# Local attention and an exact-weight MLP on one Trainium2 core: dummy transposes in planned pauses, a second buffer for late probabilities, and early transposes in another PSUM pool

## The chip, the cores and the metric

The kernel runs on one core of one Trainium2 chip. A core has a matrix engine (TensorE; PE in the profile, with its weight loads as PEld), a vector engine (VectorE, DVE), a scalar engine (ScalarE, ACT) and GpSimd (POOL). SyncE (SP) issues the DMAs. SBUF is the working memory; PSUM is the small memory that TensorE writes its results to, and here it is divided into four pools (s, o, h, a) of two buffers each. The metric is device time in microseconds; lower is better.

## The reference: what is computed

Attention over 4 batches, 8 heads, 768 positions and head size 64. Each position sees the keys less than 16 positions away, and 24 summaries of the whole sequence (the maximum of each block of 32 keys, the mean of each block of 32 values). Then layer norm and an MLP with a hidden width of 2048 are applied to the 512 joined channels, with a residual:

```python
    k_sum = k.reshape(B, H, nb, block, D).max(axis=3)
    v_sum = v.reshape(B, H, nb, block, D).mean(axis=3)
    scores_l = scale * np.matmul(q, k.transpose(0, 1, 3, 2))
    mask_l = np.abs(pos[:, None] - pos[None, :]) < window
    scores_s = scale * np.einsum('bhsd,bhnd->bhsn', q, k_sum) + np.log(block)
    scores_all = np.concatenate([np.where(mask_l, scores_l, -1e9), scores_s], axis=-1)
    a = softmax(scores_all)
    x = np.matmul(a, np.concatenate([v, v_sum], axis=2))
...
    xn = (x - mu) / np.sqrt(var + 1e-06) * g_ln
    ch = np.maximum(xn @ w_ch1, 0.0) @ w_ch2
    return (x + ch).astype(np.float32)
```

(The softmax and the joining of the heads are shortened here.) The MLP weights reach the kernel as pairs of 32-bit words, from which it rebuilds float32 values.

## The kernel before

**Tiling.** The 4 x 768 rows make 24 tiles of 128 rows. Attention works on half tiles, t = 0 to 47: four heads of one row tile each. Two row tiles make a group (12 groups), and the MLP works on groups: `g1(s)` computes 256 hidden channels of a group (24 matmuls into a PSUM tile named h) and splits the result into two float16 parts, hh (ScalarE) and hl (VectorE). `g2(s)` multiplies both parts by the second weights into accumulators named a. A float32 product is formed from float16 parts: a high part and a low remainder on each side.

**Stages.** Half tiles 0 to 11 (batch 0, `NEARLY` = 12) take an early path in float32: scores (`early_qk`, PSUM tile s), softmax, transposes of the probabilities on TensorE (`early_transp`, PSUM tile pp, copied by ScalarE to pT), the product with the values (`early_pv`, tile o), then layer norm (`ln`) and its transposed copy (`lnT`, tile tx, then xs). Meanwhile the MLP weights are decoded by `dec_w` (tiles raw and wf), scaled by `scale_w` (tiles wps and wsc) and split into float16 parts by `conv_w` (wp), mostly on VectorE and ScalarE. Half tiles 12 to 47 take the late path: float16 parts of queries, keys and values, and probabilities that are split by ScalarE and GpSimd in `transp` (p16) and transposed by DMA.

**What sets the order.** All steps are recorded by a planner (`Plan`), which knows a cost for each operation and a waiting time between engines. Nothing is written down as an order by hand: `schedule` is a list scheduler over all five engines, `improve` runs it `ROUNDS` = 32 times, forward and backward in turn, and keeps the order with the earliest planned end. `issue` then emits every instruction in order of its planned start. On the chip each engine works through its own queue in that order and waits by semaphore. The planner has a model of TensorE's clock: in ticks of 10240/3 ns it counts columns, and where a tick held fewer than 3200, matmuls take twice as long in the next one. Any change of a dependency or a cost thus lets the planner order all engines anew.

**Buffers.** A PSUM pool's two buffers are handed round in the order in which the program allocates them, so a tile has to wait until the tile two before it in its pool has been read. Pool h holds the warm-up tile, pp of half tiles 0 to 3 (`EH` = 4, two pp per half tile), then wps and the h tiles. Pool s holds the scores, and pp from half tile 4 on, and tx from row tile 2 on. Pool a holds v0, the first two tx tiles, and the accumulators. In SBUF, a work tile with the name of an older one takes its place once that one has been read. Late keys (ksg) rotate over the three places `ksg=("qke", "k0_0", "k0_1")`. Early probabilities alternate between `prob[0]` and `prob[1]`; late ones all use `prob[0]`, by this line of `softmax`:

```python
            st[t, "p"] = prob[t < NEARLY and t % 2]
```

**Lines that the steps touch.** `warm` issues 36 transposes of an identity matrix ahead of everything else (`WARM`), `early_transp` picks the pool by `t < EH`, `go_late` clears the pads of the late buffers, `transp` is what reads the late probabilities (two casts on ScalarE, two subtractions on GpSimd). In the profile every instruction carries the line of the planner's emitting loop, L349, so the tile names tell the steps apart.

Of the kernel before, what the change touches and what calls it, by code (L numbers as in the profile page):

```python
# [23 lines left out]
P = 128  # L24
# [5 lines left out]
NC = 184  # L30
NE = 192
# [4 lines left out]
NEARLY = 2 * NT  # L36
# [1 line left out]
PET = 4  # L38
HB = 9
XSCALE, W1TOP, W2TOP, SQ = 4.0, 2.0**9, 2.0**15, 2.0**-24  # L40
EH = 4
BS = 3
ROUNDS = 32
WARMQ = 4
# [8 lines left out]
RAWS += [f"w{m}" for m in range(10, 16)] + ["ring0", "ring1"] + [f"w{m}" for m in range(12, 16)]  # L53
RAWS += [f"ring{m}" for m in range(4)]
AWAY = 24
LOADS = [("fetch_k0", 0), ("fetch_k0", 1), ("fetch_q", 0), ("gain",), ("fetch_blocks",), ("fetch_k0", 2), ("fetch_k0", 3)]
LOADS += [("fetch_v0", c) for c in range(7)] + [("fetch_tail", 0), ("fetch_q", 1), ("fetch_tail", 1), ("fetch_tail", 2)]
NV = 3
HOMES = dict(
    ksg=("qke", "k0_0", "k0_1"),  # L60
    kh=("kh0", "kh1", "kx0", "kx1"),
    qs=("qs", "qw0"),
    p16=("p2", "k0_2"),
# [32 lines left out]
class Plan:  # L96
# [10 lines left out]

    def __init__(self):
        self.ops, self.slots, self.prev, self.uses = [], {}, {}, {}
        self.joined = False  # L110
        self.names, self.stage = [("", ())], 0
        for e in self.ENGINES:
            setattr(self, e, Plan.Queue(self, e))
# [125 lines left out]
    def waits(self, x):  # L239
# [7 lines left out]
                wait.append((j, self.slack(x, y) + (self.LAND.get(n, 1000) if y.engine == "sync" else self.WAIT[y.engine])))  # L247
        return wait

    def slack(self, x, y):  # L250

        name, a = self.names[x.stage]
        if x.engine == "tensor":
            if name in ("g1", "g2"):
                return SLACK2 * (a[0] >= 24)
            return SLACK * (name in ("qk", "pv", "batch_s"))
        late = name in ("load_q", "load_k", "load_v", "softmax", "transp", "pv") and a[0] >= LATE
        late |= name[:5] == "batch" and a[0] >= 2
        late |= name in ("ln", "lnT") and a[0] >= LATE // 2
        late |= name in ("g1", "g2") and a[0] >= 24  # L260
        if not late:
            return 0.0
        return SLACKD if y.engine == "sync" else SLACKE

    def schedule(self, rank, after, back):

        count = len(self.ops)
        before = [[] for _ in range(count)]
        left = [len(x) for x in after]
        for i, x in enumerate(after):  # L270
            for j, wait in x:
                before[j].append((i, wait))
        ready, start, end = [0.0] * count, [0.0] * count, [0.0] * count
        free = dict.fromkeys(self.ENGINES, 0.0)
        coming, waiting = ({e: [] for e in self.ENGINES} for _ in range(2))
        ring, warm, columns, tick = 0.0 if back else self.FIRST, False, 0.0, 0.0
        port, half = 0.0, 0
        for i in range(count):
            if not left[i]:
                heapq.heappush(coming[self.ops[i].engine], (0.0 if back else 1000.0, i))  # L280
        for _ in range(count):
            t, e = min(
                (free[e] if waiting[e] else max(free[e], coming[e][0][0]), k)
                for k, e in enumerate(self.ENGINES)
                if waiting[e] or coming[e]
            )
            e = self.ENGINES[e]
            while coming[e] and coming[e][0][0] <= t:
                i = heapq.heappop(coming[e])[1]
                heapq.heappush(waiting[e], (rank[i], i))  # L290
            i = heapq.heappop(waiting[e])[1]
            busy, moving = self.ops[i].busy, self.ops[i].moving
            if self.ops[i].port:
                t = port = max(t, port)
                port += busy
            if e == "tensor" and self.ops[i].half != half:
                t += self.SWITCH if self.ops[i].half + half != 2 or not self.ops[i].half else 0
                half = self.ops[i].half
            if e == "tensor" and not back:
                while t >= tick + self.TICK:  # L300
                    warm, columns, tick = columns >= 3200, 0.0, tick + self.TICK
                busy *= 1 if warm else 2
                at, per = t, self.ops[i].columns / busy
                while t + busy >= tick + self.TICK:
                    columns += (tick + self.TICK - at) * per
                    warm, columns, tick = columns >= 3200, 0.0, tick + self.TICK
                    at = tick
                columns += (t + busy - at) * per
            start[i], free[e], end[i] = t, t + busy, t + busy
            if e == "sync":  # L310
                ring = max(ring, t if back else t + self.SETUP) + moving
                if back:
                    free[e] = max(free[e], ring)
                end[i] = ring + (self.SETUP if back else 0)
            for j, wait in before[i]:
                ready[j] = max(ready[j], free[e] if wait is None else end[i] + wait)
                left[j] -= 1
                if not left[j]:
                    heapq.heappush(coming[self.ops[j].engine], (ready[j], j))
        return start, end  # L320

    def improve(self, rank, after, then, rounds):

        best = None
        for _ in range(rounds):
            rank = [r if x.first is None else -1e9 + x.first for r, x in zip(rank, self.ops)]
            start, end = self.schedule(rank, after, False)
            if best is None or max(end) < best[0]:
                best = max(end), start, end
            rank = [-x for x in self.schedule([-x for x in end], then, True)[1]]  # L330
        return best

    def issue(self, nc):
        for x in self.ops:
            x.first = in_front(self.names[x.stage], x.engine)
        after = [self.waits(x) for x in self.ops]
        then = [[] for _ in after]
        for i, x in enumerate(after):
            for j, wait in x:
                then[j].append((i, wait))  # L340
        rank = [0.0] * len(after)
        for i in reversed(range(len(after))):
            x = self.ops[i]
            rank[i] = min((rank[j] for j, _ in then[i]), default=0.0) - x.busy - x.moving - self.WAIT[x.engine]
        best = self.improve(rank, after, then, ROUNDS)
        self.time, self.start, self.end = best
        for _, i in sorted(zip(best[1], range(len(after)))):
            for op, a, k in self.ops[i].calls:
                getattr(getattr(nc, self.ops[i].engine), op)(*a, **k)  # L349

# [3 lines left out]
def body(ctx: ExitStack, tc, qt, qa, qe, kt, ks, va, vb, vs, g_ln, w1, w2, blocks, out):  # L354
    pl = Plan()
# [23 lines left out]
    nc = pl  # L379
# [45 lines left out]

    @pl.step
    def go_late():
        nc.gpsimd.memset(prob[0][:, :, NC:], 0.0)
        for i in range(2):
            t = late["v", i] = work(f"v16_{i}", f"v16_{i}", [P, 2, 4, 2, D], F16)  # L430
            nc.gpsimd.memset(t[:], 0.0)
# [198 lines left out]
    @pl.step  # L630
    def softmax(t, pr):
        T = t // 2
        var = 0 if T % NT == 0 else (2 if T % NT == NT - 1 else 1)
        if pr == 0:
            st[t, "p"] = prob[t < NEARLY and t % 2]
            st[t, "mn"] = work("mn", f"mn{t}", [P, 4], F32, 2)
            st[t, "sum"] = work("sum", f"sum{t}", [P, 4], F32, 2)
        p, mn, sm, ps = st[t, "p"], st[t, "mn"], st[t, "sum"], st[t, "s", pr]
        late_ = t >= NEARLY

        heads = [(2 * pr + u, 2 * pr + u, bt["mask", T // NT][:, var]) for u in range(2)] if late_ else [
            (2 * v + pr, 2 * pr + v, emask[:, var] if v else msk[:, var]) for v in range(2)
        ]
        for u, (j, i, mk) in enumerate(heads):
            w = mk.shape[1]
            nc.vector.tensor_tensor_reduce(
                p[:, i, :w], ps[:, u, :w], mk, -1.0 if late_ else -QSCALE, 3.0e38, ALU.add, ALU.min,
                mn[:, j : j + 1],
            )
        scale = -1.0  # L650
        if late_:
            m2, (scale, plus) = mn[:, 2 * pr : 2 * pr + 2], bt["c", T // NT]
            nc.gpsimd.tensor_scalar(m2, m2, plus, 0.0, ALU.mult, ALU.add)
        for j, i, mk in heads:
            x = p[:, i, : mk.shape[1]]
            nc.scalar.activation(x, x, AF.Exp, bias=mn[:, j : j + 1], scale=scale, accum_out=sm[:, j : j + 1])
# [301 lines left out]
                nc.tensor.transpose(ps[:, i % 4 * P : i % 4 * P + P], ident[:], ident[:])  # L958


    def attend(t):
        if t < NEARLY:
            early_k(t)
# [15 lines left out]
            pv(t)  # L979
        if t % 2 and t < 8:  # L980
            norm(t // 2)

    def norm(T):
        ln(T)
        lnT(T)
# [123 lines left out]
```

## Time and profile before

| what | value |
|---|---|
| median of 3 runs | 637.73 us (633.65 to 638.5) |
| the profiled execution, whole time | 638.03 us |
| the profiled execution, span of its instructions | 636.2 us |
| mean granted clock of TensorE over the span | 0.984 |
| DMA, mean over the span | 146 GB/s |

The profile is of one execution. Its span runs from the first to the last instruction; the 1.8 us by which the whole time is longer lie around it. The page gives busy time by engine and the chain of work that ended last; the answers of the trace give groups, waits, timelines and stretches. In a row of a stretch stand its length, then the busy time of PE, PEld, DVE, ACT and POOL with the number of instructions, then the granted clock of TensorE (1.00 is full speed), the DMA share and GB/s. In a timeline row stand start, duration, engine, line, operation, output and inputs by tile name, shapes and count, and in brackets the idle time before it with what ended it. In a row of waits stand the total in us, the number of times and the longest.

### The profile page before, as it was taken

Reading aid. Unit: us, or ns where it says so; the run is one execution under the profiler, and the core shown is the slowest. Engines: PE = TensorE matmul, PEld = TensorE weight load, DVE = VectorE, ACT = ScalarE, POOL = GpSimd, SP = SyncE. Lnnn points to the kernel's source line nnn. Section 1 sums busy time; section 2 is a strip of 40 time slices with the busy share of each in tenths; the row PEclk is TensorE's granted clock in tenths of the full one; section 3 lists DMA queues with packets and bytes.
Section 4 is the critical chain, followed back from the end, with each engine's and each line's share of the span. In section 5 each row is a group of like instructions: output and inputs, shape, how many; then the busy total and the mean of one; then the engine's idle time right before and its main releaser. Section 6 shows DMA issues by size and latency. Waiting matters only on the chain.

```text
span 636.2 us, 13437 instructions
## 1 busy us (share of the span) xinstructions
PE 610.9 (96%) x4611; PEld 433.3 (68%) x4611; DVE 450.8 (71%) x1190; ACT 391.5 (62%) x1036; POOL 207.8 (33%) x412
## 2 busy tenths in 40 slices
PE   8957899999999899999979999999999999999997
PEld 6746776765776676776757677677677666666665
DVE  3899889999779998878989797657447734422212
ACT  3998798888888868778877577645446531110100
POOL 4221312024455545555555354333223321100000
PEclk9988799999999999999998999999999999999999
DMA  8980487526986977798778657465335412110000
GB/s 281 349 297 22 133 280 237 183 74 165 269 194 175 216 185 187 152 254 211 192 189 177 121 141 170 116 125 125 84 93 116 102 37 60 25 51 1 18 16 34
DMA packets 124997, 93.15 MB, mean 146 GB/s; under 512 B 84864, under 2 KB 107392, under 8 KB 124928
## 3 DMA queue, kind: packets, MB, share of 16 engines
q1 hardware_dynamic: 124928, 92.29, 55.7%
q8 instruction: 36, 0.59, 0.4%
q14 instruction: 33, 0.27, 0.1%
HBM read 66.27 MB, written 6.29 MB: 114 GB/s over the span
## 4 chain that ended last, share of the span: by engine, by line
PE 52%; DVE 25%; DMA 8%; ACT 6%; POOL 4%; issue 4%; SPq 1%; DVEq 0%; ACTq 0%; POOLq 0%
PE a L349 23%; PE h L349 23%; DVE x L349 3%; DVE p L349 3%; DMA ksg<-in_kt 3%; DVE wf L349 2%; ACT p L349 2%; PE o L349 2%; DVE hl L349 2%; PE s L349 2%; POOL p L349 2%; DVE qhl L349 2%; DVE kl L349 2%; DVE v L349 2%; DVE wp L349 1%
## 5 line engine op out<-in xcount | busy, mean ns | idle before, releaser
L349 PE MATMUL h<-xs,wp 128*128 128x256 f16 x2304 | 278.2, 276 | 6.7 <-DVE hl L349 4.8
L349 PEld LDWEIGHTS <-wp 128*128 128x128 f16 x2304 | 226.7, 99 | 53.6 <-DVE hl L349 5.2
L349 PE MATMUL a<-wp,hh 128*128 128x512 f16 (+1 forms) x768 | 226.5, 377 | 0.3 <-DVE x L349 0.3
L349 PE MATMUL a<-wp,hl 128*128 128x512 f16 x384 | 144.7, 377 | 0.2 <-DVE hl L349 0.2
L349 ACT ACTIVATE hh<-h 128x512 f16<-128x512 f32 x96 | 56.6, 589 | 123.3 <-PE h L349 99.3
L349 DVE SCALAR_TENSOR_TENSOR hl<-h,hh 128x512 f16<-128x512 f32 x96 | 65.7, 685 | 86.8 <-ACT hh L349 86.6
L349 PEld LDWEIGHTS <-hh 128*128 128x128 f16 x784 | 75.3, 98 | 61.7 <-issue 0.9
L349 ACT ACTIVATE p<-p,mn,sv 128x184 f32<-128x184 f32 x144 | 76.0, 530 | 24.3 <-POOL mn L349 20.9
L349 POOL TENSOR_TENSOR p<-p,p 128x512 f16<-128x512 f32 x72 | 72.3, 1010 | 35.0 <-ACT p L349 33.2
L349 PEld LDWEIGHTS <-hl 128*128 128x128 f16 x392 | 38.3, 98 | 45.4 <-DVE hl L349 1.1
L349 DVE CUSTOM_DVE_ANT_0 p<-s,mask 128x184 f32<-128x184 f32 x144 | 42.2, 343 | 16.6 <-POOL p L349 10.0
L349 POOL TENSOR_SCALAR mn<-mn,sv 128x2 f32<-128x2 f32 x72 | 32.4, 451 | 58.3 <-DVE mn L349 57.3
L349 POOL TENSOR_TENSOR x<-x,rc 128x256 f32<-128x256 f32 x36 | 25.5, 709 | 75.5 <-DVE x L349 75.4
L349 DVE SCALAR_TENSOR_TENSOR x<-a,wsc,x 128x512 f32<-128x512 f32 (+1 forms) x48 | 35.5, 739 | 19.6 <-PE a L349 19.2
L349 ACT ACTIVATE kh<-ksg,sv 128x368 f16<-128x368 f32 x72 | 42.7, 595 | 10.0 <-POOL ksg L349 9.9
L349 DVE SCALAR_TENSOR_TENSOR kl<-ksg,sv,kh 128x368 f16<-128x368 f32 x72 | 44.5, 643 | 3.3 <-PE s L349 3.2
L349 DVE SCALAR_TENSOR_TENSOR v<-vst,sv,v 128x256 f16<-128x256 f32 x72 | 40.4, 588 | 2.3 <-ACT v L349 2.0
L349 POOL COPY ksg<-ksum 128x48 f32<-128x48 f32 x72 | 24.3, 338 | 47.9 <-DMA ksg<-in_kt 44.5
L349 DVE TENSOR_REDUCE x<-o 128x256 f32<-128x512 f32 x36 | 24.6, 685 | 16.2 <-PE o L349 15.9
L349 ACT CAST p<-p 128x512 f16<-128x512 f32 x72 | 33.1, 509 | 0.3
L349 ACT ACTIVATE v<-vst,sv 128x512 f16<-128x512 f32 x36 | 25.6, 716 | 8.8 <-PE o L349 7.2
L349 PEld LDWEIGHTS <-qhl 128*128 128x128 f16 x288 | 24.4, 99 | 5.2 <-issue 0.3
(124 smaller groups left out, 786.0 us busy)
## 6 DMA issues: line engine op xcount, KB each, us to landing
raw<-in_w SPq DMA_DIRECT2D x32, 512.0 KB
ksg<-in_kt SPq DMA_DIRECT2D x72, 184.0 KB
out_x<-x SPq DMA_DIRECT2D x23, 256.0 KB
qw<-in_qt SPq DMA_DIRECT2D x36, 128.0 KB
vst<-in_va SPq DMA_DIRECT2D x36, 128.0 KB
qs<-in_qt SPq DMA_DIRECT2D x36, 128.0 KB
vst<-in_vb SPq DMA_DIRECT2D x84, 32.0 KB
bst<-in_ks SPq DMA_DIRECT2D x12, 192.0 KB
```

The source lines that it names most:

```text
L349: getattr(getattr(nc, self.ops[i].engine), op)(*a, **k)
```

## The change

Three edits, and two that follow from them.

1. A new step `spare`, recorded once, after half tile 3: a PSUM tile of pool a and one transpose of the identity into it. In the forward schedule, from the moment at which that transpose is planned until the first planned instruction that depends on it (the tile that takes over its place in pool a), the planner fills each planned pause of TensorE. It adds transposes one after the other, 112 or 224 ns each by its clock model and counted as 256 columns, as long as more than 800 ns remain to the next planned instruction. These copies of `spare` are emitted at their planned starts. Their output is never read.
2. Late probabilities alternate between `prob[0]` and a new tile p3, which takes the place of k0_0 (batch 0's first keys). The key ring gives that place up and takes qw4 (an early query tile) as its third.
3. `EH` goes from 4 to 6: pp of half tiles 4 and 5 move from pool s to pool h.

```diff
-EH = 4
+EH = 6
+FILL_IN, FILL_END = 500, 800
-    ksg=("qke", "k0_0", "k0_1"),
+    ksg=("qke", "k0_1", "qw4"),
...
+    def watch(self):
+
+        spare = [i for i, x in enumerate(self.ops) if self.names[x.stage][0] == "spare"]
+        self.opens = spare[0] if spare else None
+        self.closes = {i for i, x in enumerate(self.ops) if self.opens in x.after}
...
             if e == "tensor" and not back:
+                if i == self.opens:
+                    opened = t
+                closed |= i in self.closes
+                at = max(free[e], opened or t)
+                while not closed and t - at > FILL_IN and t - at > FILL_END:
+                    while at >= tick + self.TICK:
+                        warm, columns, tick = columns >= 3200, 0.0, tick + self.TICK
+                    fills.append(at)
+                    at += 112 if warm else 224
+                    columns += 256
...
-        self.time, self.start, self.end = best
-        for _, i in sorted(zip(best[1], range(len(after)))):
+        self.time, self.start, self.end, fills = best
+        for _, i in sorted([*zip(best[1], range(len(after))), *((t, -1) for t in fills)]):
+            if i < 0:
+                op, a, k = self.ops[self.opens].calls[0]
+                getattr(nc.tensor, op)(*a, **k)
+                continue
...
     def go_late():
-        nc.gpsimd.memset(prob[0][:, :, NC:], 0.0)
+        late["p"] = prob[0], work("k0_0", "p3", [P, 4, NE])
+        for x in late["p"]:
+            nc.gpsimd.memset(x[:, :, NC:], 0.0)
...
-            st[t, "p"] = prob[t < NEARLY and t % 2]
+            st[t, "p"] = (prob if t < NEARLY else late["p"])[t % 2]
...
+    @pl.step
+    def spare():
+        ps = psum("a", "spare", [P, P])
+        nc.tensor.transpose(ps[:], ident[:], ident[:])
...
+        if t == 3:
+            spare()
```

More of the change, by code (lines that the diff above doesn't have):

```diff
@@ L109, in __init__ @@
         self.ops, self.slots, self.prev, self.uses = [], {}, {}, {}
-        self.joined = False
+        self.joined, self.opens, self.closes = False, None, ()
         self.names, self.stage = [("", ())], 0
@@ L276, in schedule @@
         ring, warm, columns, tick = 0.0 if back else self.FIRST, False, 0.0, 0.0
-        port, half = 0.0, 0
+        port, half, fills, opened, closed = 0.0, 0, [], None, False
         for i in range(count):
@@ L319, in schedule @@
                     heapq.heappush(coming[self.ops[j].engine], (ready[j], j))
+        if not back:
+            self.fills = fills
         return start, end
@@ L328, in improve @@
             if best is None or max(end) < best[0]:
-                best = max(end), start, end
+                best = max(end), start, end, self.fills
             rank = [-x for x in self.schedule([-x for x in end], then, True)[1]]
@@ L335, in issue @@
             x.first = in_front(self.names[x.stage], x.engine)
+        self.watch()
         after = [self.waits(x) for x in self.ops]
```

## The prediction

> **What bounds the kernel now.** I read the page first (busy shares, the chain that ended last), then busy time and granted clock by stretch, then TensorE's waits, and at each long wait the timelines of the engines behind it.
>
> ```profile
> span 636.2 us, 13437 instructions
> PE 610.9 (96%) x4611; PEld 433.3 (68%) x4611; DVE 450.8 (71%) x1190; ACT 391.5 (62%) x1036; POOL 207.8 (33%) x412
> PE 52%; DVE 25%; DMA 8%; ACT 6%; POOL 4%; issue 4%; SPq 1%; DVEq 0%; ACTq 0%; POOLq 0%
> 24.00:74.40 50.40, 37.74 (x268) 31.14 (x267) 48.33 (x145) 44.15 (x141) 11.01 (x27) 0.86 0.57 197
> 74.40:636.20 561.80, 552.06 (x4222) 386.80 (x4221) 391.31 (x1008) 334.73 (x854) 187.02 (x332) 0.99 0.55 136
> ```
>
> The last two rows (length, then busy time of PE, PEld, DVE, ACT, POOL, then clock, DMA) show two regimes. From 24 to 74.4 us VectorE is busy for 48.33 of 50.40 us and TensorE for 37.74. From 74.4 us on TensorE is busy for 552.06 of 561.80 us, so only 9.7 us of idle are left there, the tail of the output included. Time is won by starting the second regime earlier, by running TensorE faster in it, or by taking its few stalls out. The clock of 0.86 says that the first regime also has slow matmuls:
>
> ```profile
> 40.00:45.50 5.50, 0.03 (x1) 0.02 (x1) 5.06 (x13) 5.50 (x16) 1.54 (x2) 0.86 0.93 237
> 45.50:50.80 5.30, 5.29 (x26) 3.76 (x27) 5.30 (x11) 2.27 (x7) 0.00 (x0) 0.51 0.06 17
> 61.00:67.80 6.80, 5.92 (x27) 4.84 (x28) 6.55 (x15) 6.57 (x24) 0.00 (x0) 0.50 0.56 180
> 74.70:78.10 3.40, 3.40 (x18) 2.34 (x16) 3.12 (x12) 2.46 (x7) 0.92 (x1) 0.51 0.41 116
> 78.10:82.00 3.90, 3.90 (x39) 3.36 (x37) 2.47 (x4) 3.23 (x8) 1.74 (x4) 1.00 0.40 110
> 334.40:337.50 3.10, 3.08 (x16) 2.33 (x17) 3.05 (x8) 3.10 (x8) 1.84 (x3) 0.51 0.55 167
> 45.51 1.09 PE L349 MATMUL tx<-ident,xn 128*128 128x128 f32 x4 [5.48 <-DVE xn L349]
> 61.75 0.90 PE L349 MATMUL pp<-ident,p 128*128 128x128 f32 x3 [2.37 <-ACT p L349]
> 73.89 0.28 PE L349 MATMUL h<-xs,wp 128*128 128x256 f16 x1 [1.35 <-DVE hl L349]
> ```
>
> Four stretches run at half the clock: 18 matmuls fit into 3.40 us at 0.51, and 39 into 3.90 us at 1.00. Each follows a pause of TensorE: 5.48 us, 2.37 us, 1.35 us, and a late one of 3.44 us (below). What the half clock costs TensorE is half of the busy time: 5.29 x 0.49 = 2.6 us, 5.92 x 0.50 = 3.0 us, 3.40 x 0.49 = 1.7 us and 3.08 x 0.49 = 1.5 us. Only the last two lie where TensorE sets the end.
>
> **The dummies, third stretch: -1.7 us.** One transpose of the identity is planned when its PSUM slot is free, and repeated in each planned pause until 0.8 us of it are left, up to the first matmul that reuses the slot, the second accumulator of group 0, just behind 82 us (last row of the next fence). As far as planned pauses are those of the trace, they fill 4.68 + 1.57 + 0.55 = 6.8 us. Does a transpose by itself raise the clock, and how long is one? The warm-up answers it:
>
> ```profile
> 1.70 6.40 PE L349 MATMUL warm<-ident 128*128 128x128 f32 x36 [1.70 <-POOL ident masks.py:199]
> 3.00:6.40 3.40, 3.40 (x18) 3.40 (x17) 1.91 (x2) 1.81 (x3) 3.39 (x16) 1.00 0.82 239
> 6.40:8.10 1.70, 1.70 (x17) 1.57 (x15) 0.00 (x0) 0.21 (x1) 0.65 (x8) 1.00 0.97 349
> 82.21 0.60 PE L349 MATMUL a<-wp,hh 128*128 128x512 f16 x2
> ```
>
> Nothing but these 36 transposes ran, and their spacing fell from 3.40/18 = 189 ns to 1.70/17 = 100 ns (the clock column has no lower reading yet; the spacing shows the change). So transposes count as activity, and 6.8 us hold about 70 dummies. The cold stretch at 74.70 lies in TensorE's own regime, so its 1.7 us come off the end: the bounds are 0 and 1.7, and I take 1.7.
> The Trainium skill, "TensorE: Matmul & The Clock Gate", Part 4, says that the full clock does not engage for transpose-mode work. The trace differs (189 to 100 ns with transposes alone). By that rule the dummies would give nothing; that is rival C.
> The same page, "Why this matters for your kernels", tells to avoid pauses over about 3 us. By that rule alone 2.37 and 1.35 us would be harmless, this term would be zero, and the sum would come to 633.4 us; the trace differs, since the clock is 0.50 and 0.51 behind them.
>
> If the cover is gone (a planned pause at which the chip has none), the dummies stand ahead of real work; 70 x 0.10 = 7 us is the worst case, and in this regime TensorE has 50.40 - 37.74 = 12.7 us of idle to take them. I cost them at zero. The first dummy waits for the readers of an early transposed tile on ScalarE and VectorE; behind it on TensorE stand the next score and transpose matmuls. Such a wait is bounded by the 0.64 us of a row shown below; I take zero.
>
> **The dummies, first two stretches: -1.1 us.** These shorten TensorE by 2.6 + 3.0 us, but TensorE is not what is late there:
>
> ```profile
> 63.97 5.74 DMA bst<-in_ks
> 69.73 0.04 DVE kmax L349
> 73.24 0.60 DVE hl L349
> 73.83 0.61 DVE xs L349
> 74.48 6.96 PE h L349 x47
> 66.60 0.69 DVE L349 BATCH_NORM_STATS2 s<-x 128x6 f32<-128x512 f32 x1 [0.25 <-ACT x L349]
> 69.73 0.55 DVE L349 TENSOR_REDUCE kmax<-bst 128x12 f32<-128x384 f32 x1 [1.11 <-DMA bst<-in_ks]
> ```
>
> The chain into 74.48 runs through VectorE, whose only pauses in its last stretch are 0.25 and 1.11 us. With unchanged order no more than 1.36 us can be won; what is late next is VectorE's own work (hl, xs). Below zero there is no reason in the dummies. I take 1.1, the wait ahead of kmax, which a new order can fill with the normalization that a quicker TensorE delivers sooner; ends 0 and 1.4.
>
> **Six half tiles in the other PSUM pool: 0.**
>
> ```profile
> 32.26 1.18 PE L349 MATMUL s<-kx,qw 64*128 64x184 f32 x8 [0.64 <-ACT pT L349]
> 35.46 0.38 PE L349 MATMUL wps<-wacc,ones 128*128 128x4 f32 x2
> 36.67 0.82 PE L349 MATMUL pp<-ident,p 128*128 128x128 f32 x3
> 37.78 0.46 ACT L349 COPY pT<-pp 128x384 f32<-128x384 f32 x1
> ```
>
> Half tiles 4 and 5 put their transposes into pool h and leave pool s to the scores. The scores of half tile 5 then no longer wait 0.64 us for the copy of half tile 4; that is the gain. The price: pool h is handed round in program order, so the first weight scale (wps, 35.46) now has to come behind the copy of half tile 5's transposes (ends 38.24), up to 2.8 us later, and the converted weights and the first h hang on it. TensorE's pauses of 2.37 and 1.35 us before 74.48 lie behind it and cover it. Ends -0.6 and +2.8; I take 0, as VectorE's full queue decides here.
>
> **Two buffers for late probabilities: -3.5 us.** The late stage has two long stalls:
>
> ```profile
> PE h L349 <- DVE hl L349: 3.4, 1, 3.4
> PE h L349 <- DMA xs<-x: 1.6, 1, 1.6
> 334.42 2.74 PE L349 MATMUL h<-xs,wp 128*128 128x256 f16 x12 [3.44 <-DVE hl L349]
> 328.02 2.21 POOL L349 TENSOR_TENSOR p<-p,p 128x512 f16<-128x512 f32 x1
> 331.22 0.55 POOL L349 TENSOR_TENSOR rs<-rs,mhalf 128x1 f32<-128x1 f32 x1
> 331.29 0.35 DVE L349 CUSTOM_DVE_ANT_0 p<-s,mask 128x184 f32<-128x184 f32 x1 [2.08 <-POOL p L349]
> 332.46 0.57 DVE L349 TENSOR_SCALAR xn<-x,mv,rs 128x512 f32<-128x512 f32 x1
> 333.69 0.68 DVE L349 SCALAR_TENSOR_TENSOR hl<-h,hh 128x512 f16<-128x512 f32 x1
> DVE p L349 <- POOL p L349: 10.0, 8, 2.2
> ```
>
> VectorE's scores of the next half tile wait 2.08 us until GpSimd has read the single buffer; hl is queued behind them on VectorE, and TensorE behind hl. A second buffer takes that wait away: the stall shrinks to 3.44 - 2.08 = 1.36 us, and the cold stretch behind it (1.5 us) goes, together 3.5 to 3.6 us. What is late next: xn, ahead of hl in the same queue, needs rs, which ends at 331.77 on GpSimd, so with this order xn starts 332.46 - 331.77 = 0.7 us earlier at most. Ends: 0.7, and the whole stall with its cold stretch, 3.44 + 1.5 = 5.0 us. I take 3.5, the row of the wait itself. The other 7.9 us of such waits on VectorE reach TensorE in no row. GpSimd's extra memset and the third key buffer's new home are costed at zero: key buffers stay three, and GpSimd is at 33%.
>
> **Sum.** 1.7 + 1.1 + 0 + 3.5 = 6.3 us. The profiled execution took 638.03 us (636.2 of span and 1.8 around it); 638.03 - 6.3 = 631.7 us. The median of the runs shown is 637.73, and they spread from 633.65 to 638.5, so this lies 0.9% under the median. About 1% is what a measurement of this kernel can tell from no change: 631.35 and 644.1 are the bounds.
>
> **The rivals.**
> A, the forecast: 631.7 us, its own range 627.5 to 634.5.
> B, given back later: TensorE is ahead by 2.8 us after 82 us, but VectorE, ScalarE and GpSimd supply no sooner, and TensorE waits the 2.8 us at hl or for xs (3.4 and 1.6 us now). For it: those two stalls are waits for supply. Against it: these are the only long ones in more than 550 us, 5.0 us together. Only the buffers' 0.7 to 3.5 us stay: 634.5 to 637.3, say 636.
> C, the dummies do not wake the clock: only the 3.5 us stay, 634.5 us. Against it, the warm-up's spacing.
> D, slower: VectorE may run ahead into the second buffer, but its exponentials need GpSimd's mn, queued behind GpSimd's p, which took 2.21 us at 328.02. If that queue falls behind where it does not now, TensorE gets one more stall of the size of 334.42's with its cold stretch, 5.0 us, and the old one stays: 638.03 + 5.0 - 2.8 = 640.2 us. It decides from 2.8 us on; GpSimd's 33% speak against it.
> E, more: the new order also turns the 2.6 + 3.0 us of the first stretches into an earlier second regime, beyond the 1.1 counted (another 4.5 us): 627 us. VectorE's 48.33 of 50.40 us speak against it.
>
> **How the numbers follow.** A 0.50, B 0.25, C 0.03, D 0.12, E 0.10. The time is A's, 631.7. Under 631.35 lie a little over half of A (its range reaches further down, 0.27) and E (0.10): 0.37 faster. Over 644.1 lies half of D, with two such stalls: 0.06 slower. The rest, 0.57, is the same within 1%. The range reaches into E and D, 626.0 to 640.5, and leaves out about half of each, and little of A.
>
> **What would show it.** Right: granted clock 1.00 from 40 to 82 us, with dummies named spare on TensorE; 39 instead of 18 matmuls in 3.4 us where h of group 1 starts, and that start at 72 to 74 us; no wait of VectorE's p for GpSimd's p, and no stall over 2 us on TensorE behind 82 us. B shows as the same early stage with more waits for hl, xs or ACT further on; C as dummies at 0.50; D as ACT waiting for mn ahead of a stall of TensorE; a late wps as a first h behind 47 us. The forecast is wrong if the new order of all engines, planned afresh, makes or removes stalls that no row here names.

## The result, and the profile after

The changed kernel takes 633.22 us (median of 22 runs, 631.66 to 638.23) against 637.57 us before (22 runs, 633.65 to 641.75). The ratio is 0.9943 with a 95% interval of 0.9924 to 0.9961: a gain of 0.6%. The forecast was 631.7 us in a range of 626.0 to 640.5. The profiled execution took 633.28 us, 631.5 of it span. One run of e8 below (1362.76 us) and one of the kernel before (1624.43 us, beside e9 to e12) lie far outside all others, and the ratios leave them out.

From the page of the changed kernel: its span and the busy times.

```profile
span 631.5 us, 13489 instructions
PE 611.5 (97%) x4656; PEld 435.3 (69%) x4656; DVE 445.3 (71%) x1190; ACT 390.9 (62%) x1036; POOL 202.7 (32%) x413
```

TensorE's timeline of the changed kernel around the early pauses (the emitting loop is now at L373, and L370 emits the dummies):

```profile
37.34 0.39 PE L373 MATMUL wps<-wacc,ones 128*128 128x4 f32 x2
40.25 0.45 PE L373 MATMUL spare<-ident 128*128 128x128 f32 x1 [2.04 <-DVE wsc L373]
42.81 1.12 PE L373 MATMUL tx<-ident,xn 128*128 128x128 f32 x4 [0.83 <-DVE xn L373]
59.10 2.02 PE L370 MATMUL spare<-ident 128*128 128x128 f32 x17
69.84 1.36 PE L370 MATMUL spare<-ident 128*128 128x128 f32 x11
71.78 5.29 PE L373 MATMUL h<-xs,wp 128*128 128x256 f16 x47 [0.47 <-DVE wsc L373]
77.84 0.60 PE L373 MATMUL a<-wp,hh 128*128 128x512 f16 x2
```

Stretches of the changed kernel (length, busy times of PE, PEld, DVE, ACT, POOL, granted clock, DMA):

```profile
40.00:46.00 6.00, 4.92 (x20) 4.22 (x21) 5.62 (x15) 4.66 (x12) 1.81 (x3) 0.52 0.76 207
59.00:62.00 3.00, 2.40 (x22) 2.17 (x21) 3.00 (x5) 3.00 (x7) 0.00 (x0) 1.00 0.03 8
62.00:74.00 12.00, 11.30 (x101) 10.02 (x101) 11.88 (x35) 9.62 (x30) 1.80 (x4) 1.00 0.46 145
```

TensorE's waits behind 77 us in the changed kernel, and VectorE's waits for the scores there:

```profile
PE h L373 <- DVE hl L373: 1.7, 2, 1.5
PE o L373 <- DMA pT<-p: 1.6, 2, 1.3
PE h L373 <- DMA xs<-x: 1.3, 2, 0.7
PE pp L373 <- DVE mn L373: 1.0, 1, 1.0
DVE p L373 <- PE s L373: 25.9, 12, 3.6
```

The gain was made early. The first accumulator starts at 77.84 instead of 82.21 us, 4.4 us sooner, and the span is 4.7 us shorter, so behind that point only 0.3 us were won. Group 1's first h now runs at full clock: 47 matmuls in 5.29 us, where they took 6.96. The half clock behind the first long pause is still there (0.52 from 40 to 46 us): the first dummy stood waiting for 2.04 us ahead of it. Late, the stall of 3.4 us is gone, but four kinds of shorter waits sum to 5.6 us, and where VectorE's scores waited for GpSimd's reading (no such row is left), they now wait 25.9 us for TensorE's (7.9 us behind 77 us before). Of the signs that the prediction named, two held: no wait for GpSimd's p, and no stall of TensorE over 2 us. The clock of 1.00 from 40 us on did not, and group 1's h started at 71.78 us, just ahead of the named 72 to 74.

### The profile page after: what moved, and what is told of

It is laid out like the page before. It is cut to its first block, busy times and chain, and to the rows that moved or that the text cites. A ratio compares the mean times of both kernels' runs of the same rounds, so it can differ in the third digit from the quotient of the medians.

```text
span 631.5 us, 13489 instructions
## 1 busy us (share of the span) xinstructions
PE 611.5 (97%) x4656; PEld 435.3 (69%) x4656; DVE 445.3 (71%) x1190; ACT 390.9 (62%) x1036; POOL 202.7 (32%) x413
## 4 chain that ended last, share of the span: by engine, by line
PE 55%; DVE 18%; DMA 13%; ACT 4%; issue 4%; SPq 2%; POOL 2%; ACTq 0%; POOLq 0%; DVEq 0%
PE a L373 27%; PE h L373 24%; DMA ksg<-in_kt 4%; DMA raw<-in_w 3%; DMA qs<-in_qa 2%; DVE wf L373 2%; SPq L373 2%; PE o L373 2%; PE s L373 2%; DVE p L373 2%; DVE hl L373 2%; DMA bst<-in_vs 2%; DVE wp L373 2%; DVE raw L373 1%; DVE x L373 1%
## 5 line engine op out<-in xcount | busy, mean ns | idle before, releaser
L373 PE MATMUL h<-xs,wp 128*128 128x256 f16 x2304 | 272.7, 273 | 3.5 <-DVE hl L373 1.7
L373 PEld LDWEIGHTS <-wp 128*128 128x128 f16 x2304 | 223.6, 98 | 45.2 <-DVE hl L373 2.5
L373 PE MATMUL a<-wp,hh 128*128 128x512 f16 (+1 forms) x768 | 226.5, 377 | 0.0
L373 PE MATMUL a<-wp,hl 128*128 128x512 f16 x384 | 144.7, 377 | 0.0
L373 ACT ACTIVATE hh<-h 128x512 f16<-128x512 f32 x96 | 56.6, 590 | 132.1 <-PE h L373 104.3
L373 DVE SCALAR_TENSOR_TENSOR hl<-h,hh 128x512 f16<-128x512 f32 x96 | 65.6, 684 | 87.9 <-ACT hh L373 87.6
L373 PEld LDWEIGHTS <-hh 128*128 128x128 f16 x784 | 75.9, 98 | 63.2 <-issue 0.4
L373 ACT ACTIVATE p<-p,mn,sv 128x184 f32<-128x184 f32 x144 | 76.1, 530 | 19.1 <-POOL mn L373 17.9
L373 POOL TENSOR_TENSOR p<-p,p 128x512 f16<-128x512 f32 x72 | 69.4, 971 | 29.0 <-ACT p L373 26.3
L373 PEld LDWEIGHTS <-hl 128*128 128x128 f16 x392 | 38.3, 98 | 44.6
L373 DVE CUSTOM_DVE_ANT_0 p<-s,mask 128x184 f32<-128x184 f32 x144 | 43.3, 341 | 26.1 <-PE s L373 25.9
L373 ACT ACTIVATE kh<-ksg,sv 128x368 f16<-128x368 f32 x72 | 42.5, 593 | 19.2 <-POOL ksg L373 19.1
L373 POOL TENSOR_SCALAR mn<-mn,sv 128x2 f32<-128x2 f32 x72 | 31.7, 441 | 66.8 <-DVE mn L373 66.6
L373 DVE SCALAR_TENSOR_TENSOR x<-a,wsc,x 128x512 f32<-128x512 f32 (+1 forms) x48 | 35.3, 738 | 21.6 <-PE a L373 21.4
L373 DVE SCALAR_TENSOR_TENSOR kl<-ksg,sv,kh 128x368 f16<-128x368 f32 x72 | 46.1, 666 | 1.5 <-ACT kh L373 1.5
L373 POOL TENSOR_TENSOR x<-x,rc 128x256 f32<-128x256 f32 x36 | 24.9, 692 | 67.7 <-DVE x L373 63.7
L373 POOL COPY ksg<-ksum 128x48 f32<-128x48 f32 x72 | 21.5, 302 | 53.4 <-DMA ksg<-in_kt 44.0
L373 DVE SCALAR_TENSOR_TENSOR v<-vst,sv,v 128x256 f16<-128x256 f32 x72 | 38.1, 552 | 0.1
L373 ACT CAST p<-p 128x512 f16<-128x512 f32 x72 | 33.9, 504 | 0.3
L373 DVE TENSOR_REDUCE x<-o 128x256 f32<-128x512 f32 x36 | 24.5, 683 | 8.1 <-PE o L373 8.0
L373 PEld LDWEIGHTS <-pT 128*128 128x128 f16 x432 | 23.7, 98 | 7.3 <-DMA pT<-p 2.8
L373 PEld LDWEIGHTS <-qhl 128*128 128x128 f16 x288 | 24.0, 98 | 5.0
```

## The experiments

The change lets the planner make a new order of all engines, so a part tried "alone" changes two things, itself and the order. There are therefore two kinds of runs: some keep the order of another kernel instruction by instruction on every engine (kept), the others let the planner order anew (anew). Theory 1 was that the dummies make the early gain by holding the clock; theory 2, that the new order and the PSUM pool make it; rival B of the prediction, that an early gain is given back later. All ratios are to the kernel before, run beside them on the same chip.

| run | what it is | order | median us | ratio (95% interval) |
|---|---|---|---|---|
| after | the changed kernel | | 633.22 | 0.9943 (0.9924 to 0.9961) |
| e1 | after, 44 dummies left out | kept | 636.22 | 0.9969 (0.9950 to 0.9988) |
| e2 | before, 69 dummies put in | kept | 637.78 | 1.0013 (0.9991 to 1.0036) |
| e3 | before, `EH` = 6 | anew | 633.32 | 0.9949 (0.9917 to 0.9981) |
| e4 | before, two late buffers | anew | 645.12 | 1.0122 (1.0086 to 1.0157) |
| e5 | before, two late buffers | kept | 634.32 | 0.9953 (0.9925 to 0.9980) |
| e6 | e5 and the dummies of e2 | kept | 634.15 | 0.9962 (0.9937 to 0.9987) |
| e7 | before, 141 for 140 ns in the planner | anew | 644.29 | 1.0114 (1.0080 to 1.0147) |
| e8 | before, 161 for 160 ns in the planner | anew | 635.01 | 0.9962 (0.9938 to 0.9986) |
| e9 | e3 and 67 dummies | kept | 633.27 | 0.9939 (0.9912 to 0.9966) |
| e10 | e9 and two late buffers | kept | 633.43 | 0.9942 (0.9913 to 0.9971) |
| e11 | after, 141 for 140 ns in the planner | anew | 638.58 | 1.0036 (1.0013 to 1.0059) |
| e12 | after, 161 for 160 ns in the planner | anew | 631.05 | 0.9917 (0.9889 to 0.9946) |

### The dummies, in orders that are kept

**e1: the changed kernel without its dummies.** The planner plans as it did; `issue` skips the copies.

```diff
             if i < 0:
-                op, a, k = self.ops[self.opens].calls[0]
-                getattr(nc.tensor, op)(*a, **k)
                 continue
```

> The changed kernel's order on every engine, instruction by instruction, with the 44 added dummy transposes left out (the one planned one stays). If the dummies hold the clock (theory 1): the pauses at 59 to 62 and 70 to 72 us, which held 17 and 11 dummies, are followed by half clock again, group 1's first h matmuls (48, 71.0 to 77.1 us in the changed kernel) end 1.5 to 3 us later, and the time is 2 to 4 us above the changed kernel's, so 635 to 637. If the new order makes the early gain (theory 2): within 1 us of the changed kernel, 632 to 634.

Measured 636.22 us. Two stretches and three timeline rows of TensorE in e1:

```profile
59.00:62.00 3.00, 0.68 (x3) 0.68 (x4) 3.00 (x8) 3.00 (x6) 0.00 (x0) 0.72 0.01 3
62.00:68.60 6.60, 6.60 (x40) 5.52 (x40) 5.70 (x13) 3.47 (x15) 1.09 (x2) 0.61 0.63 201
63.94 6.97 PE L371 MATMUL h<-xs,wp 128*128 128x256 f16 x48
73.61 6.96 PE L371 MATMUL h<-xs,wp 128*128 128x256 f16 x47 [0.78 <-DVE wsc L371]
81.34 0.61 PE L371 MATMUL a<-wp,hh 128*128 128x512 f16 x2
```

The half clock is back in both places, group 1's 47 matmuls end at 80.57 instead of 77.07 us, and the span is 3.0 us longer (634.5). By the ratios the dummies are worth 0.26% (1.7 us), by the medians 3.0 us; the two intervals just overlap. In this order theory 1 holds. The first accumulator shows how the 4.4 us won early divide: without dummies it starts at 81.34, only 0.9 us ahead of the kernel before, and with them at 77.84. So the dummies are worth 3.5 us there, 1.83 from an earlier start of group 1's h (71.78 for 73.61) and 1.67 from its clock; behind that point 0.5 us are given back. Both profiled executions lie at the medians of their kernels (633.28 and 636.24 us).

**e2: the order before with dummies.** The planner records a transpose of no cost into the PSUM tile of the first row tile's transposes, and counts the pauses without telling its clock model, so that the order stays.

```diff
+        nc.tensor.transpose(st[0, "tx"][:, 0, :], ident[:], ident[:])
+        pl.ops[-1].busy = pl.ops[-1].columns = 0
...
+                while not closed and t - at > FILL_IN and t - at > FILL_END:
+                    fills.append(at)
+                    at += 112
```

> The kernel before, its order unchanged on every engine, with 69 dummy transposes put into its planned pauses (into the PSUM tile of the first transposed row tile). Theory 1: full clock behind the pauses of 2.4 and 1.4 us, the 48 matmuls of group 1's first h tiles end at 78.5 to 79.7 instead of 81.4 us, and the time falls by 1.7 to 2.8 us, to 635 to 636. Theory 2: the clock may rise, but VectorE's order is as it was, and the time stays within 1 us of the kernel before.

Measured 637.78 us, no gain. Stretches and TensorE's timeline of e2:

```profile
40.00:45.50 5.50, 4.61 (x43) 4.40 (x41) 5.06 (x12) 5.50 (x16) 1.53 (x2) 1.00 0.80 222
61.00:67.80 6.80, 5.65 (x50) 4.94 (x50) 6.80 (x17) 6.47 (x24) 0.12 (x1) 1.00 0.55 189
74.70:78.10 3.40, 3.40 (x33) 3.03 (x32) 2.90 (x10) 2.80 (x8) 0.70 (x1) 1.00 0.34 108
39.83 4.75 PE L367 MATMUL tx<-ident 128*128 128x128 f32 x42
73.85 5.29 PE L370 MATMUL h<-xs,wp 128*128 128x256 f16 x47 [0.31 <-DVE xs L370]
79.91 0.60 PE L370 MATMUL a<-wp,hh 128*128 128x512 f16 x2
332.09 2.74 PE L370 MATMUL h<-xs,wp 128*128 128x256 f16 x12 [3.81 <-DVE hl L370]
332.10:335.50 3.40, 3.40 (x18) 2.64 (x19) 3.35 (x8) 3.34 (x8) 2.06 (x4) 0.50 0.57 177
335.50:338.90 3.40, 3.40 (x29) 2.71 (x28) 2.70 (x12) 1.72 (x3) 2.44 (x6) 0.64 0.90 166
```

All three early half-clock stretches are gone, and the first accumulator starts 2.3 us sooner (79.91 for 82.21): 0.63 us from an earlier start of group 1's h (73.85 for 74.48) and 1.67 from their clock. Even at 332.09 the kernel is still 2.3 us ahead (334.42 before). Then the late stall, 3.81 us for 3.44, is followed by a longer half-clock stretch: 0.64 still in the second 3.4 us, where the kernel before is back at full clock from 337.5. The span ends 0.9 us ahead, and over 12 runs nothing is left. The outcome is rival B's, but in this execution most of the loss is not by its mechanism, a supply that comes no sooner: the key tile on which this stall hangs (GpSimd's copy, see e6) came 2.1 us sooner (325.05 for 327.17), the stall is only 0.4 us longer, and the longer half clock takes back about 1.4 us.

**e6: the same with two late buffers** (e5's edit, below), still in the order before.

> The same with the 69 dummy transposes of e2 as well, still in the order of the kernel before. e2 gained 2.3 us until 334 us and gave most of it back in the late stall and a longer half-clock stretch behind it. If that stall is what takes the gain (rival B): with a shorter stall the gain of 2.3 us stays, and the time lies 2 us or more below e5's. If the gain is lost whatever the stall does: within 1 us of e5.

Measured 634.15 us, as e5's 634.32: the dummies gave nothing here either. Three rows of e6, of TensorE, VectorE and GpSimd, and behind them the last one's counterpart in e5:

```profile
331.69 2.74 PE L372 MATMUL h<-xs,wp 128*128 128x256 f16 x12 [3.43 <-DVE hl L372]
329.47 0.82 DVE L372 TENSOR_SCALAR xn<-x,mv,rs 128x512 f32<-128x512 f32 x1 [1.62 <-POOL rs L372]
324.96 0.22 POOL L372 COPY ksg<-ksum 128x48 f32<-128x48 f32 x1 [3.43 <-DMA ksg<-in_kt]
324.99 0.23 POOL L350 COPY ksg<-ksum 128x48 f32<-128x48 f32 x1 [2.77 <-DMA ksg<-in_kt]
```

Read upwards from e6's last row: GpSimd waits 3.43 us for a key tile, reads the probabilities and makes rs after it; xn on VectorE waits 1.62 us for rs; hl is behind xn; TensorE waits 3.43 us for hl. e6 is 0.7 us ahead of e5 at this place (VectorE's hl before it starts at 317.84 for 318.53), but its keys are not: 324.96 for 324.99. In these two executions being ahead only meant a longer wait for a DMA of keys. e6's is one of its slow ones, though (636.82 us, with 634.15 the median), and runs of e6 with a granted clock of 1.00 over the whole span have no late half clock at all, so for the median the place of the loss is not shown.

The clock itself rises with dummies in every order that was tried. The median granted clock over all runs goes from 0.985 (before) to 0.992 (e2), from 0.986 (e5) to 0.997 (e6), from 0.984 (e3) to 0.996 (e9, next) and from 0.984 (e1) to 0.992 (the changed kernel). Only in the last pair does the median time follow clearly.

**e9: e3's order with dummies.** Edits as in e2, on e3.

> The kernel of e3 (before, with half tiles 4 and 5 in pool h, ordered anew), that order kept on every engine, with 67 dummy transposes in its planned pauses. In e3 TensorE's waits behind 77 us add up to 2.9 us and none is over 1 us, so there is little to give an early gain back to. If the dummies' gain is lost only in such stalls: group 1's h matmuls end near 77.5 instead of 80.2 us and the time falls 1.5 to 2.7 us below e3's 633.3, to 631 or 632. If VectorE's, ScalarE's and GpSimd's supply takes it back anyway: within 1 us of e3's.

Measured 633.27 us against e3's 633.32, so no gain by the medians; with 7 and 12 runs and intervals of about 0.5% this settles nothing within 2 us. The profiles differ in a way that hides it. First TensorE rows of e3, then of e9:

```profile
10.00 1.95 PE L349 MATMUL v<-vw,blk 128*120 128x512 f32 x4 [1.07 <-DMA vw<-in_va]
73.29 6.96 PE L349 MATMUL h<-xs,wp 128*128 128x256 f16 x47 [0.64 <-DVE xs L349]
```

```profile
12.03 3.13 PE L370 MATMUL v<-vw,blk 128*120 128x512 f32 x4 [3.15 <-DMA vw<-in_va]
75.78 5.29 PE L370 MATMUL h<-xs,wp 128*128 128x256 f16 x47 [0.64 <-DVE xs L370]
```

In e9's profiled execution the first value tiles arrived 2.0 us later; group 1's h began 2.5 us later, yet the span is only 0.4 us longer (631.5 for 631.1). In that execution, then, about 2 us of the lateness were made good behind 73 us, 1.67 of them by the clock of those 47 matmuls. Whether the dummies' gain stays in this order, e9 leaves open.

**e10: two late buffers on top of e9.**

> The same with the late probabilities on two buffers on the chip, order kept. In e3 VectorE waits 7.2 us for GpSimd's p, but no long stall of TensorE follows; so at most 1 us below e9's, and likely the same. A fall of 2 us or more would mean that the early gain in e9 was held back by that wait.

Measured 633.43 us: nothing for the buffers here, as expected. With e5 this says, for two orders, that the buffer pays where its wait ends in a long stall of TensorE, and not where it doesn't.

e10's profiled execution also bears on the question that e9 left: its value tiles came as early as e3's.

```profile
span 627.9 us, 13544 instructions
9.80 1.95 PE L372 MATMUL v<-vw,blk 128*120 128x512 f32 x4 [1.20 <-DMA vw<-in_va]
72.01 5.29 PE L372 MATMUL h<-xs,wp 128*128 128x256 f16 x47 [0.64 <-DVE xs L372]
```

Group 1's h ends at 77.30, 2.95 us sooner than in e3 (80.25), and the span is 3.2 us shorter (627.9 for 631.1). Between these two executions, then, the early gain stayed. But e10's is one of its fastest (630.44 us, with 633.43 the median), and the medians of e3, e9 and e10 show no gain, so the question stays open.

### The late buffers, order kept and anew

**e5: two buffers in the order before.** The planner is told that both buffers are one tile and plans as before; the chip sees two. The key ring's second place lies in an old query tile on the chip. The line of `softmax` is the changed kernel's.

```diff
+                tile = self.alias.get(tile, tile)
...
+        late["p"] = prob[0], work("p3", "p3", [P, 4, NE], at="k0_0")
+        pl.alias[late["p"][1].tensor.name] = prob[0].tensor.name
...
...
```

> The kernel before, its order unchanged on every engine, with the late probabilities on two buffers on the chip (the planner still plans with one; the key ring's second place moves to another old query tile). One GpSimd memset more. If the wait for the buffer is what makes the late stall (the prediction's term): VectorE's waits for GpSimd's p go from 10.0 us to 0, the 3.4 us stall near 331 us shrinks by 0.7 to 2.1 us, the half clock behind it may go (1.5 us), 634 to 636.5 in all. If something else comes last there (rival): the stall stays within 0.5 us and the time within 1 us of the kernel before. A time well above the kernel before's would mean that two buffers cost something by themselves.

Measured 634.32 us, 3.3 us under the kernel before by the medians. TensorE's row at the late stall, the stretch behind it, VectorE's remaining wait for scores, and group 1's h, in e5:

```profile
331.22 1.48 PE L350 MATMUL h<-xs,wp 128*128 128x256 f16 x12 [2.24 <-DVE hl L350]
331.20:334.60 3.40, 3.38 (x35) 3.11 (x36) 2.91 (x8) 3.40 (x10) 1.58 (x3) 1.00 0.75 210
DVE p L350 <- PE s L350: 9.5, 9, 3.2
74.61 0.28 PE L350 MATMUL h<-xs,wp 128*128 128x256 f16 x1 [1.45 <-DVE hl L350]
75.21 5.29 PE L350 MATMUL h<-xs,wp 128*128 128x256 f16 x47 [0.31 <-DVE xs L350]
```

The waits for GpSimd's p have no row any more, the stall is 2.24 instead of 3.44 us, and the matmuls behind it take 1.48 instead of 2.74 us, at full clock. The profiled span is 4.7 us shorter, and not all of that is the buffers': in this execution group 1's 47 matmuls ran at full clock too (5.29 us), without a dummy and behind a pause of 1.45 us. The stall and the 12 matmuls behind it account for 1.2 + 1.26 = 2.5 us.

**e4: the same part, ordered anew.**

> The kernel before with the second buffer for late probabilities (and the key ring's new place) as the only edit, ordered anew. The prediction: VectorE's waits for GpSimd's p (10.0 us) go, the stall of 3.4 us near 331 us and the half clock behind it go, 3.5 us less, 634. Rival B: the waits come back elsewhere as waits for scores, xs or pT, TensorE's waits behind 78 us stay near 6 us, and the time is within 1.5 us of the kernel before.

Measured 645.12 us, 7.8 us slower, a miss for both expectations. TensorE's timeline of e4:

```profile
47.47 1.09 PE L349 MATMUL tx<-ident,xn 128*128 128x128 f32 x4 [4.75 <-DVE xn L349]
79.49 4.77 PE L349 MATMUL h<-xs,wp 128*128 128x256 f16 x27 [0.83 <-DVE xs L349]
```

The late buffers are used from half tile 12 on, but here group 1's h starts 5 us later than before (79.49 for 74.48). That is not the work of the late buffer itself: e5 has the same buffers in the kept order and starts it at 75.21. Ordering anew moved the early stage. (1.0 us of it may be this execution's later value tiles, at 11.23 for 10.24; it took 647.64 us.)

### The PSUM pool, and what an order is worth

**e3: `EH` = 6 alone, ordered anew** (the one-line edit).

> The kernel before with half tiles 4 and 5's transposes in pool h as the only edit, ordered anew by the planner. Theory 2: row tile 2's transposes (tx, 45.5 us before, 42.8 in the changed kernel) come 2 us or more earlier, group 1's first h starts near 72 instead of 73.9 us, and the time falls by 2 to 3 us. Theory 1 and the prediction: no gain from this part, within 1 us of the kernel before.

Measured 633.32 us, as fast as the whole change. TensorE's row of tx, and its longest wait behind 77 us, in e3:

```profile
41.33 1.12 PE L349 MATMUL tx<-ident,xn 128*128 128x128 f32 x4 [4.50 <-DVE xn L349]
PE a L349 <- DVE x L349: 1.0, 1, 1.0
```

The transposes of row tile 2 come 4.2 us sooner (45.51 before), group 1's h 1.2 us sooner (73.29 for 74.48), and no late stall is longer than 1.0 us. So most of this gain lies in a late stage, far behind the transposes that the edit moves. How much belongs to the pool and how much to the order, e3 can't tell; e7 and e8 show why.

**e7 and e8: the kernel before, with one planner number moved by 1 ns.**

```diff
-    WAIT = dict(tensor=200, vector=140, scalar=160, gpsimd=90, sync=1000)
+    WAIT = dict(tensor=200, vector=141, scalar=160, gpsimd=90, sync=1000)
```

(e8 has scalar=161 instead.)

> The kernel before with nothing changed but one number of the planner, the waiting time behind VectorE, 141 instead of 140 ns; the order differs on every engine behind the first matmuls. It measures what ordering anew does by itself. If a new order is worth little: within 1 us of the kernel before. If it is worth as much as the parts of the change showed (e3 4 us less, e4 8 us more): 3 us or more off, either way.

> The same with the waiting time behind ScalarE, 161 instead of 160 ns. Expected as for e7; two such orders that differ by several us from each other would show that a part ordered anew can't be told from its order by its time alone.

Measured 644.29 and 635.01 us. The same work in three orders takes 635.0, 637.6 and 644.3 us. e7's longest wait of TensorE behind 77 us:

```profile
185.77 1.25 PE L349 MATMUL o<-v,pT 128*128 128x128 f16 x12 [3.19 <-DMA pT<-p]
```

**e11 and e12: the same for the changed kernel.**

> The changed kernel with the planner's waiting time behind VectorE at 141 instead of 140 ns, ordered anew. Orders of the kernel before lay at 637.5, 644.3 and 635.0 us. If the changed kernel's 633.2 is mostly the luck of its order: 2 us or more off it, likely above, 635 to 641. If the three parts themselves make it: 632 to 635.

> The changed kernel with the planner's waiting time behind ScalarE at 161 instead of 160 ns, ordered anew. Expected as for e11.

Measured 638.58 and 631.05 us. The long stall of e11, GpSimd's wait ahead of it, and group 1's h in e12:

```profile
289.98 2.74 PE L373 MATMUL h<-xs,wp 128*128 128x256 f16 x12 [4.40 <-DVE hl L373]
287.86 0.22 POOL L373 COPY ksg<-ksum 128x48 f32<-128x48 f32 x1 [7.70 <-DMA ksg<-in_kt]
71.33 5.29 PE L373 MATMUL h<-xs,wp 128*128 128x256 f16 x47 [0.39 <-DVE wsc L373]
```

e11 has a stall of 4.40 us with half clock behind it, of the kind that the kernel before had at 334 us, in spite of two buffers. e12 has none over 0.8 us and is the fastest median of all, 631.05, though its interval overlaps the changed kernel's. Compared at the same planner number, the change gives -4.4 us (140 and 160), -5.7 (141) and -4.0 (161). By the ratios, each to the kernel before in its own measurement, that is 3.6, 5.0 and 2.9 us. Three pairs, all of one sign, point to 3 to 6 us for the three parts together; but they are few, as the order alone moves either kernel by 7 to 9 us.

## Why the prediction was right, point by point

**The time and its sign** came out (633.2 for 631.7), but by other terms than those of the sum: 4.4 us were won early where 2.8 were forecast, and 0.3 us late where 3.5 were. That the two errors nearly cancel is luck, and so is the order that the planner found: with 1 ns more in one of its numbers the changed kernel takes 638.6 or 631.1 us. Of the 4.7 us of profiled span, e1 puts 3.0 down to the dummies; no run divides the other 1.7 among the order, the pool and the buffers.

**Dummies, third stretch, -1.7 us: right in mechanism and size.** The 47 matmuls went from 6.96 to 5.29 us, 1.67 us, in the changed kernel and in e2 and e9. What the step left out is whether the gain stays. In the order before the medians show none of it (e2, e6); in the changed kernel's order it stays (e1: 1.7 to 3.0 us are lost without it). Rival B had the outcome right for one order and wrong for the other; its mechanism, no sooner supply, was the smaller part of e2's loss. The count, about 70, was 69 in e2; the changed kernel's new order needed 45.

**Dummies, first two stretches, -1.1 us:** with VectorE's order kept, e2 measured 0.63 us, within the ends of 0 and 1.4. In the changed kernel's order it was 1.83 us (e1), beyond the upper end, so part of what rival E named came true.

**The first dummy's own wait, costed at zero with 0.64 as bound:** mis-sized. It waited 2.04 us for readers on VectorE, and the first half-clock stretch stayed. e1 has the same wait, and nothing isolates its cost in time. In e12 the first dummy waits only 0.58 us, and the granted clock is 1.00 from 40 to 82 us (0.92 in the changed kernel).

**Six half tiles in pool h, 0:** the price was right (wps at 37.34 for 35.46, 1.9 us later). The first h came at 47.35 for 46.40 us, past the 47 us named as the sign of a late wps, but group 1's h did not start later for it. The step failed where it said that VectorE's full queue decides: the new order found room, tx came 2.7 us sooner in the changed kernel and 4.2 in e3. Of that, where no dummies help, only 0.9 us (e1) and 1.2 us (e3) reached group 1's h. As to the time, e3 is 4.0 us faster, mostly in the late stage, which the step had no term for.

**Two late buffers, -3.5 us:** right when nothing else moves (e5: 3.3 us by the medians, the stall shrinking by 1.2 instead of the 2.08 taken, the half clock gone). In the changed kernel the late stage gained only 0.3 us: with a new order, waits for pT, xs and scores took the place of the one removed. The step worked out that xn, behind rs, could start only 0.7 us earlier, and then took 3.5 all the same. In e5 that limit did not hold: GpSimd's subtraction ahead of rs took 1.16 us instead of 2.21, rs ended at 328.96, and xn started at 329.00 without a wait. In e6 it did hold: xn waited 1.62 us for rs.

**What the sum had no term for** is the order itself. It stood as the last sentence of the prediction; e7, e8, e11 and e12 put a size on it, larger than any term of the sum.

**Rival C** fell: e2's and the changed kernel's transposes hold the clock at 1.00. **Rival D** did not show in the changed kernel, but e11 shows a price like D's: one stall of 4.40 us with half clock. What stands behind it is not D's wait for mn but keys: GpSimd waits 7.70 us for a key tile by DMA.

## What to carry to other kernels

Where a planner orders everything anew, time a few neutral changes of it first (one number by 1 ns): their spread, 7 to 9 us here, is the yardstick for a part of the change, and a part has to be tried in a kept order before its time says anything about its mechanism. A gain ahead of a stall can be lost in it, by a supply that comes no sooner (e6's keys) or by the half clock behind it (e2). Dummy matmuls are cheap protection for the clock, but plan for their own waits: the first of them stood 2 us behind readers of the PSUM tile whose place it takes.

## What the runs showed of the hardware

Float32 transposes of an identity alone keep TensorE at full clock: in e2, 42 of them ran for 4.75 us in a pause (113 ns each), and the stretch from 40.0 to 45.5 us is at 1.00, where it was 0.86 and led into 0.51 before. The Trainium skill, "TensorE: Matmul & The Clock Gate", Part 4, says that transpose-mode work does not engage the full clock; the trace differs, and the measurement decides. (The profile lists these transposes as MATMUL and does not show in which mode they ran.)

A pause need not be long to bring the half clock: pauses of 2.37 and 1.35 us did before the change, and 0.68 us of work in 3.00 us did in e1 (0.72 of full clock from 59 to 62, then 0.61). Nor does its length alone decide: in e5's execution 1.45 us at the place of the 1.35 did not. When the half clock comes and goes shows in the kernel before:

```profile
43.91:50.74 6.83, 5.23 (x25) 3.73 (x26) 6.39 (x13) 3.79 (x13) 0.88 (x1) 0.50 0.21 54
60.97:67.80 6.83, 5.92 (x27) 4.84 (x28) 6.58 (x15) 6.60 (x24) 0.00 (x0) 0.50 0.55 179
74.63:78.05 3.42, 3.42 (x18) 2.36 (x17) 3.19 (x11) 2.41 (x7) 0.92 (x1) 0.50 0.40 115
334.04:337.46 3.42, 3.04 (x16) 2.29 (x17) 3.34 (x9) 3.42 (x10) 2.16 (x3) 0.50 0.63 174
```

These are all the half-clock stretches of its span. They last 6.83 or 3.42 us, and their starts lie 17.06, 13.66 and 259.41 us apart: 2, 1, 5, 4 and 76 times the planner's tick of 3.413 us. So in this execution the clock changed only on a fixed grid, which fits a cost of a pause that depends on where it falls in that grid. In the last 3.41 us ahead of 74.63 TensorE was busy for 1.74 us and the half clock followed; in e5's stretch from 71.34 to 74.76 us it was busy for 1.97 us and it did not.

Executions differ by when the first value tiles land. e3 and e9 run the same instructions up to there, yet TensorE waited 1.07 us for the tiles in e3's profiled execution and 3.15 in e9's, with group 1's h 2.5 us later. The changed kernel's 22 runs spread over 6.6 us, more than its gain.
